# Order of the first transfers and of the first steps in a kernel for sliding-window attention and an ELU feed-forward layer

## The chip, the cores and the metric

The kernel runs on one core of a Trainium2 chip. The metric is the device time of one execution in microseconds (us), as the median of several executions; lower is better. In what follows PE is TensorE (matrix products and transposes), PEld its weight loads, DVE is VectorE, ACT is ScalarE, POOL is GpSimd and SP is SyncE. SP and ACT also issue transfers of the hardware queues, POOL those of the software queue, which may change the type on the way.

## What is computed

Attention with a window of 32 to each side, on 8 batches of 8 heads, 576 positions, head size 64; its output, laid out as 4608 tokens by 512, goes through a feed-forward layer of width 2048 with ELU.

```python
scores = scale * np.matmul(q, k.transpose(0, 1, 3, 2))
mask = np.abs(pos[:, None] - pos[None, :]) <= window
scores = np.where(mask, scores, -1000000000.0)
attn = np.exp(scores - np.max(scores, axis=-1, keepdims=True))
attn = attn / (np.sum(attn, axis=-1, keepdims=True) + 1e-09)
x = np.matmul(attn, v)        # then to (4608, 512)
h = x @ w_in
g = np.where(h > 0.0, h, alpha * (np.exp(np.minimum(h, 0.0)) - 1.0))
out = g @ w_out
```

## The kernel before

All inputs and the output are float32 in HBM; the products run in bfloat16. The kernel has two halves that run interleaved, in an order written out by hand: every engine executes its instructions in the order in which the Python code emits them.

**Attention.** The 576 queries of a batch are nine blocks of 64; two blocks are a "pair" of 128 tokens, so there are 36 pairs. For a pair, `scores` (L281) makes 16 products of keys and queries into PSUM, `exponential` (L296) is one activation on ACT into the tile `pu`, `mask` (L303) a multiplication on DVE with 0/1 masks into `pm`, `pv` (L312) 16 products with the values, `normalize` (L326) a reciprocal and a multiplication on DVE into `x_st`, `x_transpose` (L337) four transposes on PE and `x_evac` (L353) their eviction by ACT into `xT`. The values stand in `V_e`, with an extra column of ones that gives the row sums, and shifted by 64 positions in `V_o`, which `rotate_v` (L137) copies on DVE.

**Queries and keys** must be transposed. `load_qk` (L115) loads them, in halves of a batch (HALF_A, HALF_B; four transfers of 288 KB for q and k together, two of them for each) or whole. `cast_qk` (L236) casts to bfloat16, `transpose_qk` (L266) transposes on PE into PSUM and evicts to `qT` or `kT`. For batch 0, `front_cast` and `front_transpose` (L367, L371) do this in two pieces. HALF_A of batch 0 serves pairs 0 and 1, HALF_B pairs 2 and 3.

**Feed-forward layer.** Two pairs make a tile of 256 tokens; there are 18 tiles and 8 groups of 256 hidden units each, so 144 steps. `mm1(kk)` (L544, "first product of step kk") multiplies w_in with `xT` (eight matmuls of 128x256), ACT takes the exponential (`e_sb`, L565), DVE subtracts one (`m_sb`, L567), and one step later `elu` (L572) makes `g_sb`. `mm2(kk)` (L583, "second product of step kk") multiplies `g_sb` with w_out into PSUM, four matmuls of 128x512. By `order` (L539) steps 0 to 3 take tile 0 and hidden groups 0 to 3, steps 4 to 7 tile 1 and the same groups; steps 8 on take groups 4 to 7. The weights are loaded in quarters by `load_w_in` and `load_w_out` (L153, L160) on POOL's queue, which casts them; quarter c holds groups 2c and 2c + 1. So steps 0 and 1 need quarter 0, step 2 is the first that needs quarter 1, step 8 the first that needs quarter 2.

**Order at the start.** POOL makes the identity and the masks, then issues V's blocks 1, 0, 2 of batch 0, three last mask operations, w_in quarter 0, V's blocks 3 and 4, w_out quarter 0 and so on. SP issues HALF_A of batch 0 (with ACT), then stands at a gate: `gate` (L148) is a transfer of one element whose only purpose is that SP waits until its source is written, here the last mask. After it come the loads of HALF_B, then a gate on w_in's quarter 1, the loads of HALF_A of batch 1, a gate on w_in's quarter 3, and the further loads. On PE `idle` (L376) emits products with zeros in places where PE would wait.

**Loop.** From L609 on, each step kk runs `elu(kk - 1)`, the tasks of slot "dve", `mm1(kk)`, the tasks of slot "mid", the second products (normally of step kk - 2, LAG at L608; exceptions in the table at L618), and the tasks of slot "end". The tasks of the first steps (L452 to L465) hold the transposes of HALF_B and pairs 2 and 3; `swap_pools` at step 4 gives PSUM space of the first pairs to later tiles.

Of the kernel before, what the change touches and what calls it, by code (L numbers as in the profile page):

```python
# [10 lines left out]
BF16 = mybir.dt.bfloat16  # L11
# [4 lines left out]
def _bap(ap, new_ap, off=0):  # L16
    return bass.AP(tensor=ap.tensor, offset=ap.offset + off,
                   ap=[list(x) for x in new_ap])
# [3 lines left out]
def kernel(  # L22
# [9 lines left out]
    nc = tc.nc  # L32

    B, H, S, D = q.shape
# [9 lines left out]
    HP = H // 2  # L44
    NC = 128 // HP
# [69 lines left out]
    def load_qk(b, which, part, engs=(nc.sync, nc.sync)):  # L115
        z, nj = part
        t = lpool.tile([128, 2, nj * D], FP32, tag=f"f{which}{nj}",
                       name=f"f{which}")
        qk_f[b, which, z] = t
        src = (q, k)[which][b, :, z * NC * nj:(z + 1) * NC * nj, :].rearrange(  # L120
            "(g h) (c j) d -> c g h (j d)", h=2, j=nj)
        for h in range(2):
            engs[h].dma_start(out=t[:, h, :], in_=src[:, :, h, :])  # L123

    def load_v(b, m):
        lo = 128 * m - WIN
        p0 = max(0, -lo)
        p1 = min(128, S - lo)
        nc.gpsimd.dma_start(  # L129
            out=V_e[b % 3][p0:p1, m, :, 0:D],  # L130
            in_=v[b, :, lo + p0:lo + p1, :].rearrange("h p d -> p h d"))
# [16 lines left out]
    def gate(src, dt=BF16, eng=nc.sync):  # L148
        gates[0] += 1
        t = cpool.tile([1, 1], dt, name=f"gate{gates[0]}")  # L150
        eng.dma_start(out=t, in_=src)

    def load_w_in(c):  # L153
        w = D_FF // 4
        nc.gpsimd.dma_start(
            out=w_in_sb[:, :, c * w:(c + 1) * w],
            in_=moe_w_in[:, c * w:(c + 1) * w].rearrange(
                "(o p) f -> p o f", p=128))

    def load_w_out(c):  # L160
        n = NFO // 4
        nc.gpsimd.dma_start(
            out=w_out_sb[:, c * n:(c + 1) * n, :],
            in_=moe_w_out[c * n * 128:(c + 1) * n * 128, :].rearrange(
                "(o p) f -> p o f", p=128))

    def w_in_at(c):
        return w_in_sb[0:1, 0, (c + 1) * (D_FF // 4) - 1:(c + 1) * (D_FF // 4)]
# [7 lines left out]
    def edges(i):  # L176
        nc.vector.memset(V_e[i][:, :, :, D:VD], 1.0)
        nc.vector.memset(V_e[i][0:32, 0], 0.0)
        nc.vector.memset(V_e[i][96:128, VS - 1], 0.0)
        if i < 2:  # L180
            for c0, n in ((KPAD - WIN, HP), (KPAD + HP * S, 1)):
                z = kT[i][:, c0:c0 + WIN]
                nc.vector.memset(_bap(z, [z.ap[0], [S, n], [1, WIN]]), 0.0)

    edges(0)
    edges(1)

    ident = cpool.tile([128, 128], BF16)
    make_identity(nc, ident)

# [7 lines left out]
        base=2 * WIN, pattern=[[0, 5], [1, QB]], channel_multiplier=-1)  # L200
    for m in (1, 0, 2):
        load_v(0, m)
    for mi in (0, 4):
        nc.gpsimd.affine_select(
            out=masks[:, mi, :], in_=masks[:, mi, :], compare_op=ALU.is_ge,
            fill=0.0, base=-WIN, pattern=[[0, QB]], channel_multiplier=1)
# [3 lines left out]
        channel_multiplier=-1)  # L210
    kinds = ["FE", "EE", "EL", "LF"]

    gate(masks[0:1, 3, 0:1])
    for which in range(2):
        load_qk(0, which, HALF_B)
    load_w_in(0)
    for m in (3, 4):
        load_v(0, m)
    load_w_out(0)
    load_w_in(1)  # L220
    load_w_out(1)

# [7 lines left out]
    def copy_on(eng, d_, s_):  # L230
        if eng is nc.scalar:
            nc.scalar.copy(d_, s_)  # L232
        else:
            eng.tensor_copy(d_, s_)  # L234
# [12 lines left out]
    def keys_or_queries(b, which):  # L247
        if which == 0:
            return qT[b % 2].rearrange("p g s -> p (g s)")
        return kT[b % 2][:, KPAD:KPAD + HP * S]  # L250
# [12 lines left out]
        nc.sync.dma_start_transpose(  # L263
            out=keys_or_queries(b, which), in_=in_dram.pop((b, which)))

    def transpose_qk(b, which, part, j0, n, evac, tag="t0"):  # L266
        z, nj = part
        src = qk_b[b, which, z]
        pt = ps_tile([128, 1024 if n <= 8 else 2048], BF16, tag, "ptx")
        for j in range(n):  # L270
            nc.tensor.transpose(  # L271
                pt[:, j * 128:(j + 1) * 128], src[:, j0 + j, :], ident)
        d = keys_or_queries(b, which)
        copy_on(evac,
                _bap(d, [d.ap[0], [S, HP], [nj, NC], [1, n]],
                     z * NC * nj + j0),
                _bap(pt, [pt.ap[0], [1, HP], [HP, NC], [128, n]]))

    st = {}

# [15 lines left out]
    def exponential(i):  # L296
        psS = st[i][0]
        pu = apool.tile([128, H, 2 * QB], BF16, tag="pu")
        nc.scalar.activation(  # L299
            pu, _bap(psS, [psS.ap[0], [1, 1024]]), AX.Exp, scale=SCALE)  # L300
        st[i][1] = pu
# [35 lines left out]
    def x_transpose(i):  # L337
        x_st, tag = st[i][3:]
        pt = ps_tile([128, NDO, 128], BF16, tag, "psXT")
        for do in range(NDO):  # L340
            nc.tensor.transpose(
                pt[:, do, :], x_st[:, 2 * do:2 * do + 2, :], ident)
        st[i] = pt
# [9 lines left out]
    def x_evac(i, eng=nc.vector):  # L353
        copy_on(eng, xT_of(i), st.pop(i))
# [12 lines left out]
    def front_cast(which, part, eng):  # L367
        for j0, n in SPLIT:
            cast_qk(0, which, part, j0, n, eng)

    def front_transpose(which, part, evac, tags):  # L371
        for (j0, n), tag in zip(SPLIT, tags):
            transpose_qk(0, which, part, j0, n, evac, tag)


    def idle(n, tag):  # L376
        ps = ps_tile([128, 512], FP32, tag, "ps_idle")
        for _ in range(n):
            nc.tensor.matmul(ps, lhsT=zeros[:, 0:128], rhs=zeros,
                             start=True, stop=True)  # L380
# [12 lines left out]
    for i, tag in ((0, "s"), (1, "u")):  # L393
        scores(i, tag)
        exponential(i)
    idle(4, "y0")
    rotate_v(0, 0, 2)
    for i in (0, 1):
        mask(i)
    pv(0)  # L400
    idle(2, "h0")
    pv(1)
    for i in (0, 1):
        normalize(i)
    for i in (0, 1):
        idle(1, "h1")
        x_transpose(i)
        x_evac(i, nc.scalar)
    idle(2, "h1")
    front_cast(0, HALF_B, nc.scalar)  # L410
    front_cast(1, HALF_B, nc.vector)


    load_w_in(2)
    load_w_out(2)
    for m in range(3):
        load_v(1, m)
    load_w_in(3)
    load_w_out(3)
    for m in range(3, VS):  # L420
        load_v(1, m)
    gate(w_in_at(1))
    for which in range(2):
        load_qk(1, which, HALF_A)
    gate(w_in_at(3))
# [10 lines left out]
    def at(kk, slot, fn, *args):  # L436
        tasks.setdefault((kk, slot), []).append((fn, args))
# [11 lines left out]
        at(kk + 2, "end", x_evac, i, nc.scalar)  # L449


    at(1, "mid", front_transpose, 1, HALF_B, nc.scalar, ("s", "u"))  # L452
    at(1, "mid", front_transpose, 0, HALF_B, nc.vector, ("y0", "y1"))
    at(2, "dve", rotate_v, 0, 2, VS - 1)
    for i, tag in ((2, "s"), (3, "u")):
        at(1, "mid", scores, i, tag)
        at(1, "mid", exponential, i)
        at(2, "dve", mask, i)
    at(2, "dve", lambda: mm2(1))
    for i in (2, 3):  # L460
        at(2, "dve", pv, i)
        at(2, "dve", normalize, i)
        at(3, "mid" if i == 3 else "dve", x_transpose, i)
        at(3, "mid" if i == 3 else "dve", x_evac, i, nc.scalar)
    at(4, "dve", swap_pools)  # L465

    for part, kq in ((HALF_A, 7), (HALF_B, 15)):
# [115 lines left out]
    def mm2(kk):  # L583
        t, s = order[kk]
        if s == 0:
            psY[t] = [ps_tile([128, D_MODEL], FP32, g, "psY")
                      for g in (("h2", "t0") if t == 1 else ("y0", "y1"))]
        g_sb = g_t.pop(kk)
        last = t == NT - 1 and s == STEPS - 1
        for ts in range(2):  # L590
            for j in range(FG):
                nc.tensor.matmul(  # L592
                    psY[t][ts],
                    lhsT=g_sb[:, j, ts * 128:(ts + 1) * 128],
                    rhs=w_out_sb[:, s * FG + j, :],
                    start=(s == 0 and j == 0),
                    stop=(s == STEPS - 1 and j == FG - 1))
        if s == STEPS - 1:
            for ts in range(2):
                z = 1 - ts if last else ts  # L600
                eng = (nc.scalar, nc.vector)[z]
                y_sb = opool.tile([128, D_MODEL], FP32, tag=f"y_sb{z}",
                                  name="y_sb")
                copy_on(eng, y_sb, psY[t][ts])
                (nc.scalar if last and ts else nc.sync).dma_start(
                    out_t[t, :, ts, :], y_sb)

    LAG = 2  # L608
    for kk in range(NSTEP + LAG):  # L609
        run(kk, "first")  # L610
        if 1 <= kk < NSTEP:
            elu(kk - 1)
        run(kk, "dve")
        if kk < NSTEP:
            mm1(kk)
        run(kk, "mid")

        for n in {1: (0,), 2: (), 3: ()}.get(  # L618
                kk, (kk - LAG,) if kk >= LAG else ()):
            mm2(n)  # L620
        run(kk, "end")
# [30 lines left out]
```

The softmax here doesn't subtract the row's maximum and nothing guards it: scores larger than these inputs give would overflow.

## Time and profile before

The median of 13 executions is 312.81 us (311.62 to 315.13). The profile was taken of the execution that lasted 315.13 us, whose span is 313.4 us; the rest lies around the span.

| engine | busy, us | share of the span |
|---|---|---|
| PE | 294.8 | 94% |
| DVE | 246.9 | 79% |
| ACT | 170.7 | 54% |
| POOL | 43.8 | 14% |

| stretch, us | PE busy, us | granted clock of PE | DMA, GB/s |
|---|---|---|---|
| 10 to 15 | 4.42 | 0.90 | 260 |
| 15 to 20 | 3.38 | 1.00 | 218 |
| 20 to 25 | 2.66 | 0.63 | 206 |
| 25 to 30 | 5.00 | 0.69 | 227 |
| 30 to 35 | 4.01 | 1.00 | 267 |
| 60 to 80 | 19.34 | 1.00 | 205 |
| 160 to 240 | 78.13 | 1.00 | 164 |

Some times of the first steps, from the timeline: the first product of step 0 starts at 15.48 us, of step 2 at 27.65, of step 4 at 31.16, of step 6 at 34.63. SP's gate on the masks goes at 6.39, the four loads of HALF_B from 7.19 on; the gate on w_in's quarter 1 at 24.30, the loads of HALF_A of batch 1 from 25.03 on. POOL issues w_in quarter 0 at 6.33, w_out quarter 0 at 8.96, w_in quarter 1 at 9.71. How to read the lines that follow: in the chain of waits a line is a start, a length and what the time went to; in a timeline it is start, busy time, engine, line of the code, operation, the tile written and the tile read, and in brackets how long the engine was idle before and what ended that; in a table of stretches it is the stretch, then busy time (and count) of PE, PEld, DVE, ACT and POOL, the granted clock, the DMA engines' share and GB/s.

### The profile page before, as it was taken

To read this page: it belongs to the slowest core of one execution; us is meant where nothing else is said; L and a number is where in the kernel's file an instruction comes from. 1 tells how busy PE (TensorE), PEld (TensorE's weight loads), DVE (VectorE), ACT (ScalarE), POOL (GpSimd) and SP (SyncE) were. 2 spreads that over 40 slices of the span, in tenths; PEclk is the share of its full clock that TensorE was granted. 3 is DMA by queue.
4 is the path that set the end of the run, shared out by engine and by line. 5 is a ranking of instruction groups with operands and counts; after the bars stand their busy time and mean duration, and the time that the engine had idled before them with its cause. 6 is when DMAs were issued, how large, how long until landed. Compare 5 with 4: busy or idle time off the path is not lost.

```text
span 313.4 us, 7510 instructions
## 1 busy us (share of the span) xinstructions
PE 294.8 (94%) x2996; PEld 198.2 (63%) x3048; DVE 246.9 (79%) x480; ACT 170.7 (54%) x256; POOL 43.8 (14%) x60
## 2 busy tenths in 40 slices
PE   6858999999999999999998999999999999999994
PEld 2445666667666666666665666666666666666662
DVE  6666688799979788888886888888888787776663
ACT  3554556868683775567366735673636353534331
POOL 8633000572102032020202000000000000000000
PEclk9787999999999999999999999999999999999998
DMA  9999999999999999779999996269111111111011
GB/s 189 222 205 239 223 231 356 299 195 188 332 197 173 339 187 176 221 94 255 269 137 168 389 252 159 62 191 188 69 36 67 36 69 35 69 33 69 0 69 68
DMA packets 91657, 52.93 MB, mean 169 GB/s; under 512 B 76518, under 2 KB 80614, under 8 KB 91622
## 3 DMA queue, kind: packets, MB, share of 16 engines
q1 hardware_dynamic: 48022, 36.77, 44.2%
q0 software_dynamic: 41728, 8.92, 38.4%
q10 hardware_dynamic: 1872, 6.75, 6.6%
q8 instruction: 24, 0.39, 0.6%
q14 instruction: 11, 0.09, 0.1%
HBM read 36.70 MB, written 15.34 MB: 166 GB/s over the span
## 4 chain that ended last, share of the span: by engine, by line
PE 81%; DVE 7%; DMA 4%; issue 2%; POOL 2%; ACT 1%; SPq 1%; DVEq 0%; POOLq 0%
PE ps L558 37%; PE psY L592 36%; PE psS L288 3%; PE psS L320 3%; DMA f<-in_k_dram 3%; DVE g_sb L577 2%; DMA xT<-x_st 2%; PE ptx L271 1%; DVE m_sb L567 1%; DVE pm L308 1%; DVE x_st L332 1%; POOL Ve L129 1%; SPq L123 1%; ACT e_sb L565 1%; DVE y_sb L234 1%
## 5 line engine op out<-in xcount | busy, mean ns | idle before, releaser
L565 ACT ACTIVATE e_sb<-ps 128x512 f32<-128x512 f32 (+1 forms) x145 | 86.2, 594 | 122.7 <-PE ps L558 115.5
L558 PE MATMUL ps<-xT,w_in_sb 128*128 128x256 bf16 x1152 | 149.5, 273 | 2.9 <-DVE g_sb L577 1.6
L592 PE MATMUL psY<-w_out_sb,g_sb 128*128 128x512 bf16 x525 | 140.6, 383 | 3.2 <-issue 0.9
L558 PEld LDWEIGHTS <-w_in_sb 128*128 128x128 bf16 x1152 | 110.8, 98 | 41.7 <-issue 3.5
L577 DVE SCALAR_TENSOR_TENSOR g_sb<-ps,m_sb 128x512 bf16<-128x512 f32 (+1 forms) x145 | 99.5, 686 | 12.9 <-PE ps L558 0.5
L567 DVE TENSOR_SCALAR m_sb<-e_sb 128x512 bf16<-128x512 f32 (+1 forms) x145 | 62.7, 433 | 32.7 <-ACT e_sb L565 30.8
L592 PEld LDWEIGHTS <-g_sb 128*128 128x128 bf16 x576 | 54.9, 98 | 39.3 <-issue 1.6
L129 POOL DMA_DIRECT2D Ve<-in_v_dram x40 | 34.9, 887 | 136.2 <-PE psS L320 96.8
L299 ACT ACTIVATE pu<-psS 128x1024 bf16<-128x1024 f32 x36 | 36.5, 1020 | 4.0 <-PE psS L288 4.0
L332 DVE TENSOR_TENSOR x_st<-psS,rc 128x512 bf16<-128x512 f32 x36 | 24.9, 692 | 3.4 <-DMA xT<-x_st 2.2
L232 ACT CAST qkb<-f 128x768 bf16<-128x768 f32 (+3 forms) x32 | 26.7, 837 | 0.0
L308 DVE TENSOR_TENSOR pm<-pu,masks 128x1024 bf16<-128x1024 bf16 x36 | 24.6, 683 | 1.5 <-ACT pu L299 1.5
L320 PEld LDWEIGHTS <-pm 128*64 128x64 bf16 x576 | 11.4, 113 | 10.2 <-DVE pm L308 6.8
L288 PE MATMUL psS<-qT,kT 64*128 64x64 bf16 x576 | 12.7, 196 | 2.6 <-DVE qT L234 2.1
L140 DVE COPY Vo<-Ve 64x1040 bf16<-64x1040 bf16 x32 | 14.2, 444 | 1.0
L288 PEld LDWEIGHTS <-kT 64*128 64x128 bf16 x576 | 10.3, 98 | 7.2 <-issue 5.4
L320 PE MATMUL psS<-Ve,pm 128*64 128x65 bf16 x320 | 13.9, 199 | 0.3 <-DVE pm L308 0.2
L234 DVE COPY y_sb<-psY 128x512 f32<-128x512 f32 x18 | 12.3, 686 | 1.2 <-PE psY L592 1.1
L320 PE MATMUL psS<-Vo,pm 128*64 128x65 bf16 x256 | 12.6, 199 | 0.2 <-DVE pm L308 0.2
L234 DVE CAST qkb<-f 128x1152 bf16<-128x1152 f32 (+3 forms) x14 | 8.5, 627 | 4.9 <-DMA f<-in_k_dram 4.4
L232 ACT COPY y_sb<-psY 128x512 f32<-128x512 f32 x18 | 10.5, 583 | 2.2 <-PE psY L592 2.2
L271 PE MATMUL ptx<-ident,qkb 128*128 128x128 bf16 x108 | 8.4, 225 | 3.2 <-DVE qkb L234 3.2
(32 smaller groups left out, 65.9 us busy)
## 6 DMA issues: line engine op xcount, KB each, us to landing
out_dram<-y_sb SPq DMA_DIRECT2D x35, 256.0 KB, 2.6
f<-in_q_dram SPq DMA_DIRECT2D x12, 576.0 KB, 8.8
f<-in_k_dram SPq DMA_DIRECT2D x12, 576.0 KB, 8.9
in_dram<-qkb ACTq DMA_DIRECT2D x10, 576.0 KB, 5.2
Ve<-in_v_dram POOLq DMA_DIRECT2D x24, 128.0 KB, 7.7
w_in_sb<-in_moe_w_in_dram POOLq DMA_DIRECT2D x4, 512.0 KB, 16.3
w_out_sb<-in_moe_w_out_dram POOLq DMA_DIRECT2D x4, 512.0 KB, 17.5
f<-in_q_dram SPq DMA_DIRECT2D x7, 288.0 KB, 6.0
```

What stands on the lines that cost most here:

```text
L129: nc.gpsimd.dma_start(out=V_e[b % 3][p0:p1, m, :, 0:D], in_=v[b, :, lo + p0:lo + p1, :].rearrange("h p d -> p h d"))
L232: nc.scalar.copy(d_, s_)
L288: nc.tensor.matmul(psS[:, h % 2, hp * 128 + z * QB:hp * 128 + (z + 1) * QB], lhsT=kT[b % 2][base:base + 64, KPAD + hp * S + QB * qb - WIN: ...
L299: nc.scalar.activation(pu, _bap(psS, [psS.ap[0], [1, 1024]]), AX.Exp, scale=SCALE)
L308: nc.vector.tensor_mul(pm, pu, _bap(mm, [mm.ap[0], [0, H], [1, 2 * QB]]))
L320: nc.tensor.matmul(psS[QB * z:QB * (z + 1), par, hp * VD:(hp + 1) * VD], lhsT=pm[:, par * HP + hp, z * QB:(z + 1) * QB], rhs=vv[:, qb // 2 ...
L332: nc.vector.tensor_mul(x_st, _bap(psS, [psS.ap[0], [VD, HP], [512, 2], [1, D]]), _bap(rc, [rc.ap[0], [2, HP], [1, 2], [0, D]]))
L558: nc.tensor.matmul(ps[:, j, :], lhsT=w_in_sb[:, do, fo * 128:(fo + 1) * 128], rhs=xT[t][:, :, do, :], start=(do == 0), stop=(do == NDO - 1))
L565: nc.scalar.activation(e_sb, ps, AX.Exp)
L567: nc.vector.tensor_scalar(m_sb, e_sb, -1.0, None, ALU.add)
L577: nc.vector.scalar_tensor_tensor(g_t[kk][:, z * w:(z + 1) * w, :], ps, 0.0, m_t[kk][z], ALU.max, ALU.min)
L592: nc.tensor.matmul(psY[t][ts], lhsT=g_sb[:, j, ts * 128:(ts + 1) * 128], rhs=w_out_sb[:, s * FG + j, :], start=(s == 0 and j == 0), stop=( ...
```

## The change

- The identity is made ahead of the memsets of V and kT in the code; on each engine alone the order stays.
- SP's first gate waits for the last memset of kT (DVE) in place of the last mask operation (POOL); the four loads of HALF_B of batch 0 stand behind it.
- POOL issues w_in quarter 0 ahead of the three last mask operations, w_out quarter 0 ahead of V's blocks 3 and 4, and V's blocks 0 and 1 of batch 1 ahead of w_in's quarter 2.
- SP's second gate, ahead of HALF_A of batch 1, waits for the first exponential (`pu` of pair 0) in place of w_in's quarter 1.
- The casts and transposes of HALF_B go ahead of step 0: q's casts stand ahead of the xT evictions on ACT, q's transposes between those of pairs 0 and 1 on PE, with evictions on ACT (before: DVE) deferred behind both xT evictions; k's transposes follow, with evictions on DVE (before: ACT).
- Five of the twenty products with zeros are left out.
- The value products of pairs 2 and 3 go behind the first product of step 2; their normalization goes to step 3, their transposes around the second product of step 2.
- Second products 2 and 3 run in steps 3 and 4 (before: 4 and 5).

```diff
@@ -182,11 +182,16 @@
                 z = kT[i][:, c0:c0 + WIN]
                 nc.vector.memset(_bap(z, [z.ap[0], [S, n], [1, WIN]]), 0.0)
 
+    ident = cpool.tile([128, 128], BF16)
+    make_identity(nc, ident)
+
+
+
     edges(0)
     edges(1)
-
-    ident = cpool.tile([128, 128], BF16)
-    make_identity(nc, ident)
+    gate(kT[1][0:1, KPAD - 1:KPAD])
+    for which in range(2):
+        load_qk(0, which, HALF_B)
 
 
 
@@ -200,6 +205,7 @@
         base=2 * WIN, pattern=[[0, 5], [1, QB]], channel_multiplier=-1)
     for m in (1, 0, 2):
         load_v(0, m)
+    load_w_in(0)
...
@@ -210,13 +216,9 @@
         channel_multiplier=-1)
     kinds = ["FE", "EE", "EL", "LF"]
 
-    gate(masks[0:1, 3, 0:1])
-    for which in range(2):
-        load_qk(0, which, HALF_B)
-    load_w_in(0)
+    load_w_out(0)
     for m in (3, 4):
         load_v(0, m)
-    load_w_out(0)
     load_w_in(1)
     load_w_out(1)
 
...
@@ -263,18 +265,25 @@
         nc.sync.dma_start_transpose(
             out=keys_or_queries(b, which), in_=in_dram.pop((b, which)))
 
-    def transpose_qk(b, which, part, j0, n, evac, tag="t0"):
+    def transpose_qk(b, which, part, j0, n, evac, tag="t0", later=None):
         z, nj = part
         src = qk_b[b, which, z]
         pt = ps_tile([128, 1024 if n <= 8 else 2048], BF16, tag, "ptx")
         for j in range(n):
             nc.tensor.transpose(
                 pt[:, j * 128:(j + 1) * 128], src[:, j0 + j, :], ident)
-        d = keys_or_queries(b, which)
-        copy_on(evac,
-                _bap(d, [d.ap[0], [S, HP], [nj, NC], [1, n]],
-                     z * NC * nj + j0),
-                _bap(pt, [pt.ap[0], [1, HP], [HP, NC], [128, n]]))
+
+        def evict():
+            d = keys_or_queries(b, which)
+            copy_on(evac,
+                    _bap(d, [d.ap[0], [S, HP], [nj, NC], [1, n]],
+                         z * NC * nj + j0),
+                    _bap(pt, [pt.ap[0], [1, HP], [HP, NC], [128, n]]))
+
+        if later is None:
+            evict()
+        else:
+            later.append(evict)
 
...
@@ -368,9 +377,9 @@
         for j0, n in SPLIT:
             cast_qk(0, which, part, j0, n, eng)
 
-    def front_transpose(which, part, evac, tags):
+    def front_transpose(which, part, evac, tags, later=None):
         for (j0, n), tag in zip(SPLIT, tags):
-            transpose_qk(0, which, part, j0, n, evac, tag)
+            transpose_qk(0, which, part, j0, n, evac, tag, later)
...
@@ -393,33 +402,39 @@
     for i, tag in ((0, "s"), (1, "u")):
         scores(i, tag)
         exponential(i)
+    st0 = st[0][1]
     idle(4, "y0")
     rotate_v(0, 0, 2)
     for i in (0, 1):
         mask(i)
     pv(0)
-    idle(2, "h0")
+    idle(1, "h0")
     pv(1)
     for i in (0, 1):
         normalize(i)
-    for i in (0, 1):
-        idle(1, "h1")
-        x_transpose(i)
-        x_evac(i, nc.scalar)
-    idle(2, "h1")
     front_cast(0, HALF_B, nc.scalar)
+    evictions = []
+    x_transpose(0)
+    x_evac(0, nc.scalar)
+    front_transpose(0, HALF_B, nc.scalar, ("y0", "y1"), evictions)
+    x_transpose(1)
+    x_evac(1, nc.scalar)
+    for evict in evictions:
+        evict()
     front_cast(1, HALF_B, nc.vector)
-
-
+    front_transpose(1, HALF_B, nc.vector, ("s", "u"))
+
+
+    for m in (0, 1):
+        load_v(1, m)
     load_w_in(2)
     load_w_out(2)
-    for m in range(3):
-        load_v(1, m)
+    load_v(1, 2)
     load_w_in(3)
     load_w_out(3)
     for m in range(3, VS):
         load_v(1, m)
-    gate(w_in_at(1))
+    gate(st0[0:1, 0, 0:1])
     for which in range(2):
         load_qk(1, which, HALF_A)
     gate(w_in_at(3))
...
@@ -449,19 +464,16 @@
         at(kk + 2, "end", x_evac, i, nc.scalar)
 
 
-    at(1, "mid", front_transpose, 1, HALF_B, nc.scalar, ("s", "u"))
-    at(1, "mid", front_transpose, 0, HALF_B, nc.vector, ("y0", "y1"))
+    at(2, "dve", lambda: mm2(1))
     at(2, "dve", rotate_v, 0, 2, VS - 1)
     for i, tag in ((2, "s"), (3, "u")):
         at(1, "mid", scores, i, tag)
         at(1, "mid", exponential, i)
         at(2, "dve", mask, i)
-    at(2, "dve", lambda: mm2(1))
-    for i in (2, 3):
-        at(2, "dve", pv, i)
-        at(2, "dve", normalize, i)
-        at(3, "mid" if i == 3 else "dve", x_transpose, i)
-        at(3, "mid" if i == 3 else "dve", x_evac, i, nc.scalar)
+        at(2, "mid", pv, i)
+        at(3, "dve", normalize, i)
+        at(3, "mid" if i == 2 else "end", x_transpose, i)
+        at(3, "mid" if i == 2 else "end", x_evac, i, nc.scalar)
     at(4, "dve", swap_pools)
...
@@ -615,7 +627,7 @@
             mm1(kk)
         run(kk, "mid")
 
-        for n in {1: (0,), 2: (), 3: ()}.get(
+        for n in {1: (0,), 2: (), 3: (2,), 4: (3,), 5: ()}.get(
                 kk, (kk - LAG,) if kk >= LAG else ()):
             mm2(n)
         run(kk, "end")
```

## The prediction

> **What bounds the kernel now.** I read the page first: TensorE (PE) is busy 94% of the span and reads 9 tenths in almost every slice, except the first three (6, 8, 5). What can be won or lost by an edit of the first transfers lies there. Next the chain of waits from 9 us on:
>
> ```profile
> 9.89 8.30 DMA f<-in_k_dram
> 18.19 0.02 issue
> 18.22 0.83 DVE qkb L234 x2
> ...
> 20.72 1.36 DVE qT L234 x2
> 22.08 0.04 issue
> 22.12 1.04 PE psS L288 x32
> 23.16 0.54 PE psY L592
> ...
> 26.69 1.03 PE psS L320 x29
> 27.71 1.20 PE ps L558 x8
> ```
>
> The end hangs on the last load of the second half of k: it lands at 18.2 us, is cast, transposed and evicted until 22.1, and only then do the scores of pairs 2 and 3 (L288) go, after them the second products of steps 0 and 1 (L592), the value products (L320), and at 27.65 the first product (L558) of step 2. Third, GpSimd's (POOL's) own timeline, because its waits tell when the weights land: the bracket names the transfer that released it.
>
> ```profile
> 15.28 0.79 POOL L129 DMA_DIRECT2D Ve<-in_v_dram  x1 [2.58 <-DMA w_in_sb<-in_moe_w_in_dram]
> ...
> 22.05 0.75 POOL L155 DMA_DIRECT2D w_in_sb<-in_moe_w_in_dram  x1 [0.68 <-DMA w_out_sb<-in_moe_w_out_dram]
> 24.57 0.74 POOL L162 DMA_DIRECT2D w_out_sb<-in_moe_w_out_dram  x1 [1.76 <-DMA w_in_sb<-in_moe_w_in_dram]
> 27.11 0.88 POOL L129 DMA_DIRECT2D Ve<-in_v_dram  x1 [1.80 <-DMA w_out_sb<-in_moe_w_out_dram]
> ```
>
> So quarter 0 of w_in is there by about 15, quarter 0 of w_out by about 21.8, quarter 1 of w_in by 24.3 (SP's gate on it goes at 24.30), quarter 1 of w_out by 27. Step 2 is the first to use quarter 1 of w_in: it has 27.65 - 24.3 = 3.3 us of slack, no more. Fourth, the DMA queues over 19 to 28 us, when only GpSimd's queue (q0) moves, and over 29 to 33 us, when the loads of q and k (q1, issued by SP) run beside it:
>
> ```profile
> q0 software_dynamic: 1872, 1.86, 124.3%
> ...
> q1 hardware_dynamic: 490, 1.02, 75.3%
> q0 software_dynamic: 552, 0.21, 42.2%
> ```
>
> (packets, MB, share of 16 engines). Alone q0 moves 1.86 MB in 9 us, 206 GB/s; beside q1 0.21 MB in 4 us, 52 GB/s. A load of q and k stops the weights almost entirely. Last, the granted clock in stretches around the idle time:
>
> ```profile
> 17.86:21.27 3.41, 1.23 (x18) 1.10 (x19) 2.94 (x6) 1.53 (x3) 1.65 (x2) 1.00 1.32 202
> 21.27:24.70 3.43, 2.36 (x35) 1.46 (x36) 2.92 (x6) 1.93 (x2) 0.98 (x3) 0.50 1.24 206
> 24.70:28.10 3.40, 3.40 (x40) 1.75 (x39) 1.42 (x3) 0.01 (x1) 1.49 (x2) 0.50 1.24 206
> ```
>
> After a stretch in which PE works 1.23 of 3.41 us, its clock is 0.50 for the next two.
>
> [...]
>
> **The change, part by part.** I follow one mark: the start of the first product of step 6, at 34.63 us in the timeline of before. There both kernels have the same products behind them (first products 0 to 5, second products 0 to 3), and from there on the order is the same on every engine.
>
> 1. *Second half of q and k earlier.* SP's gate waited for the last mask operation and went at 6.39; now it waits for the last memset of kT, which ends at about 4.6. The four loads go some 1.7 us earlier, and meet V's small packets rather than w_in in the queue: before, q1 moved only the gate's 2 packets between 8.5 and 11 us although its loads were issued from 7.19. I expect k to land at 14.5 to 16 instead of 18.2.
>
> 2. *Its transposes ahead of step 0.* 18 transposes (1.23 us) and the casts (0.83 on DVE, 1.25 on ACT, which now stand ahead of the two xT evictions in ACT's order) go before the first product of step 0. Before, that product started at 15.48, on the xT eviction. Now, with k landed at about 14.6: cast to 15.4, transposes to 16.2; at 16.2 to 17 step 0 starts, 0.7 to 1.5 us later. Then steps 0 and 1 (1.91), scores (1.04), and second products 0 and 1 (4 x 0.215 us each at full clock, 1.75 for both): if nothing else held it, step 2 could start at 16.2 + 4.7 = 20.9, not 27.65. The eviction of qT that stood behind m_sb and g_sb on DVE (20.64 to 22.07) is out of the way.
>
> 3. *Gate of batch 1's first half: pu of pair 0 instead of quarter 1 of w_in.* The first exponential ends at about 11.0, so these four loads (1.18 MB) are issued from 11.7 instead of 25.03, and stand in q1 right behind the second half of batch 0. In the queues of the chip they are now ahead of the end of w_in quarter 0, of w_out quarter 0, V's blocks 3 and 4, and w_in quarter 1. Price: over 28.5 to 34.5 us, where they ran before, q0 moved 0.47 MB in 6 us; at 206 GB/s it would have been 1.24 MB. The 0.77 MB are 3.7 us; as part of it is V, slower by itself, I take 3.2 (bounds 3.0 and 3.7). On the credit side w_in quarter 0 is issued 0.9 us earlier (5.4 instead of 6.33) and the stretch from 8.5 to 11 us, where q0 moved only 0.31 MB (125 GB/s, 1.0 us short of its own pace), is filled by q1. I take 0.9 (bounds 0 and 1.4). Quarter 1 of w_in then lands at 24.3 + 3.2 - 0.9 = 26.6 (25.9 to 28.0). Call it T: step 2 starts at T, 5.7 us after PE could have.
>
> 4. *w_out quarter 0 ahead of V's blocks 3 and 4.* It lands at 20.5 to 23.5, V at 23 to 25 by the same reckoning; second products, rotation (0.88) and masks (2 x 0.69) end before T or with it. Cost nothing while T is the last; if V came 2 us later, the value products would be held by that.
>
> 5. *After T.* The value products of pairs 2 and 3 now stand behind the first product of step 2, and their normalization behind g_sb of step 2 on DVE. With the latencies of the timeline (first product to end of g_sb: 31.16 to 34.08, 2.92): g_sb of step 2 ends at T + 2.92; reciprocal and x_st of pair 2 0.94, of pair 3 0.85: T + 4.7. Transposes of pair 2 0.3, second product of step 2 0.86, transposes of pair 3 to about T + 5.45, eviction on ACT to T + 6.1, where step 4, which reads this xT, begins. From step 4 to step 6 before took 3.47 with two second products; one of these (0.86) is already done, but step 6 needs the bank that g_sb of step 4 frees, 2.95 after step 4's start. The mark is at T + 9.05; before it was 27.65 + 6.98.
>
> 6. *Clock.* PE idles before T (about 22.5 to 26.6), so the stretch after it is granted half: the first product and value products at half cost 0.2 to 0.4 more; I take 0.3. Five warm-up products less (L379) cost nothing by themselves.
>
> 7. *V of batch 1 (blocks 0, 1) before quarter 2 of w_in.* It moves that quarter to about T + 6.6 = 33.2; its first use is step 8, after 38. Nothing.
>
> Sum: 26.6 + 9.05 + 0.3 = 35.95 against 34.63: 1.3 us slower. Against the profiled execution's own 315.13 us (span 313.4) this is 316.4; that execution was the slowest of the 13, 2.3 above their median, so at the median it is 312.81 + 1.3 = 314.1. Bounds of T, 25.9 and 28.0, give +0.6 and +2.7; without the clock term +0.3: 313.1 to 315.5.
>
> **Rivals.** *The weights land in time.* The mark equals that of before at T = 34.63 - 9.05 = 25.6; below it the change wins. If q1 has so much of its work done in the poorly used stretch before 11 us, or takes its turns so, that quarter 1 of w_in keeps its old place or comes 0.9 earlier (24.3 to 23.4), the mark is at 33.35 to 32.45: 1.3 to 2.2 faster, 311.5 to 310.6. For it: the long wait for k is removed without doubt, and SP's loads can't have cost q0 what it didn't use. Against it: the two queue lines, and that the sum of bytes ahead of quarter 1 grows by 1.18 MB. *The loads of batch 1 start late* (before, q1's loads first moved 3.5 to 4 us after their issue, 7.19 to about 11.3 and 25.03 to about 28.5): then half of their cost falls behind quarter 1, T is about 25, and the time is 0.3 to 0.6 faster, about 312.4: no change. *V is hit.* If SP's earlier loads hold back V's first blocks, rotation, masks and step 0 come later; it would take 5 us of it before it shows, as T comes last. Price 0 until then; 1 us for each above.
>
> **How the numbers follow.** Forecast (weights late) 0.60, weights in time 0.30, loads late 0.10. A measurement of this kernel can tell about 0.3%, 0.94 us, from no change. Of the forecast's 0.60 about 0.52 lie above +0.94 and 0.08 within; of the second 0.28 faster, 0.02 within; of the third 0.05 faster, 0.04 within, 0.01 slower. Together 0.33 faster, 0.14 same, 0.53 slower. Range: from 310.6 (the second rival's better end) to 315.8, the forecast's end and 0.3 for the clock's chance; the forecast's own is 313.1 to 315.5.
>
> **What would show it.** Right: GpSimd's waits show quarter 1 of w_in landing at 26 to 28; PE's first product of step 2 waits for it with PE idle for over 2 us before; k's second half lands before 16; q1 is busy from about 8 to 20 us. Wrong: step 2 starts before 25.6, or waits for V or masks rather than for w_in; then the queue's sharing, step 3 of the sum, is what failed.

## The result, and the profile after

The changed kernel takes 314.69 us (median of 11 runs, 313.80 to 315.34), the kernel before, run beside it, 312.55 (48 runs, 310.66 to 315.13): a ratio of 1.0069 with a 95% interval of 1.0047 to 1.0090. It is 2.1 us slower. The profiled execution took 315.23 us (span 313.5).

The page of the changed kernel, its engine line, the engine shares of its chain, and the row of the first products (the last column is PE's idle time ahead of them and what ended most of it):

```profile
PE 292.6 (93%) x2990; PEld 197.1 (63%) x3043; DVE 246.9 (79%) x480; ACT 170.5 (54%) x256; POOL 44.1 (14%) x60
...
PE 83%; DMA 5%; DVE 5%; POOL 3%; issue 2%; ACT 1%; DVEq 0%; POOLq 0%
...
L570 PE MATMUL ps<-xT,w_in_sb 128*128 128x256 bf16 x1152 | 151.0, 275 | 4.7 <-DMA w_in_sb<-in_moe_w_in_dram 3.3
```

PE is as busy as before, to one per cent; the reader should look at the end of the last line: 3.3 of the 4.7 us are one wait for a quarter of w_in. The chain of waits of the changed kernel from 9.7 us on shows where it stands:

```profile
9.71 16.18 DMA w_in_sb<-in_moe_w_in_dram
25.90 0.05 issue
25.94 1.89 PE ps L570 x8
27.83 1.03 PE psS L329 x31
28.86 1.82 PE ps L570 x8
30.68 0.55 PE psXT L350 x4
```

In the kernel before this stretch hung on the second half of k; now it hangs on quarter 1 of w_in, which lands at 25.89, and the first product of step 2 (25.94) follows 0.05 us later. PE's own timeline of the changed kernel (bracket: idle before, and what ended it):

```profile
20.80 1.89 PE L604 MATMUL psY<-w_out_sb,g_sb 128*128 128x512 bf16 x7 [1.43 <-DMA w_out_sb<-in_moe_w_out_dram]
25.94 1.89 PE L570 MATMUL ps<-xT,w_in_sb 128*128 128x256 bf16 x8 [3.26 <-DMA w_in_sb<-in_moe_w_in_dram]
...
28.79 1.89 PE L570 MATMUL ps<-xT,w_in_sb 128*128 128x256 bf16 x8
...
36.27 1.03 PE L570 MATMUL ps<-xT,w_in_sb 128*128 128x256 bf16 x8 [0.20 <-DVE g_sb L589]
```

The last line is the mark, the first product of step 6, at 36.27 us. The two 1.89 are first products of 8 matmuls at a granted clock of 0.50 (25.0 to 31.6 us); at 1.00 they take 1.03 to 1.05. The second half of k, which the kernel before waited for until 18.2, is there early, as DVE's timeline of the changed kernel shows:

```profile
15.77 0.83 DVE L236 CAST qkb<-f 128x640 bf16<-128x640 f32 x2 [1.89 <-DMA f<-in_k_dram]
```

SP's queue and GpSimd's timeline of the changed kernel, one fence each, show what stands ahead of that weight:

```profile
10.11 0.63 SPq L151 DMA_DIRECT2D gate<-pu  x1
10.84 1.20 SPq L123 DMA_DIRECT2D f<-in_q_dram  x2
```

```profile
21.04 0.74 POOL L162 DMA_DIRECT2D w_out_sb<-in_moe_w_out_dram  x1 [5.08 <-DMA w_out_sb<-in_moe_w_out_dram]
23.81 1.11 POOL L129 DMA_DIRECT2D Ve<-in_v_dram  x1 [2.03 <-DMA Ve<-in_v_dram]
24.91 0.76 POOL L155 DMA_DIRECT2D w_in_sb<-in_moe_w_in_dram  x1
26.18 0.74 POOL L162 DMA_DIRECT2D w_out_sb<-in_moe_w_out_dram  x1 [0.51 <-DMA w_in_sb<-in_moe_w_in_dram]
```

The gate on pu lets batch 1's first loads of q and k go from 10.84. Quarter 0 of w_out is there at about 21, V's last blocks at about 23.8, quarter 1 of w_in by 25.9. The queues of the changed kernel over 11 to 20 us (packets, MB, share of 16 engines):

```profile
q1 hardware_dynamic: 881, 1.81, 59.2%
q0 software_dynamic: 932, 0.82, 55.1%
```

GpSimd's queue moves 0.82 MB in 9 us, 91 GB/s, against 206 when it was alone (the kernel before, 19 to 28 us). The two queues moved about as many packets in this stretch, 881 and 932; a packet of q1 is 2054 B and one of q0 880 B (bytes over packets), so q and k got more than twice the bytes. Not every stretch shows equal counts: in the kernel before q1 had 382 packets over 13 to 16 us and q0 828, of about 160 B, with 0.78 and 0.13 MB. That q and k took the larger part of the bytes is measured in both. Last, the granted clock (third number from the right) in the stretches of the changed kernel that the prediction looked at:

```profile
17.86:21.27 3.41, 1.92 (x43) 1.43 (x42) 2.54 (x5) 3.02 (x4) 0.23 (x1) 1.00 1.50 268
21.27:24.70 3.43, 1.42 (x6) 0.45 (x5) 1.08 (x3) 0.00 (x0) 1.40 (x2) 1.00 1.41 201
24.70:28.10 3.40, 2.16 (x20) 1.38 (x22) 1.06 (x2) 0.23 (x1) 1.71 (x3) 0.53 1.67 186
```

The idle time falls into the second stretch and the half clock into the third, in which step 2 starts.

One more reading is needed before anything is compared. The two profiled spans, 313.4 and 313.5, are nearly equal, although the medians differ by 2.1. The waits of the kernel before over steps 60 to 80 (147.85 to 187.58 us; total, times, longest) name one part of the reason:

```profile
DVE x_st L332 <- DMA xT<-x_st: 2.2, 2, 1.4
```

That stretch took 39.73 us there and 38.33 in the changed kernel. The wait is not in every execution: the kernel before profiled again (e0, below) doesn't show it over 146 to 185 us, and takes 279.2 us from the mark to its time, against 280.5. So the profile of before that the prediction was made from has about 1.3 us in it, far behind the mark, that the second profile doesn't have.

### The profile page after: what moved, and what is told of

It reads as the page before. It is cut to its first block, busy times and chain, and to the rows that moved or that the text cites. A ratio compares the mean times of both kernels' runs of the same rounds, so it can differ in the third digit from the quotient of the medians.

```text
span 313.5 us, 7500 instructions
## 1 busy us (share of the span) xinstructions
PE 292.6 (93%) x2990; PEld 197.1 (63%) x3043; DVE 246.9 (79%) x480; ACT 170.5 (54%) x256; POOL 44.1 (14%) x60
## 4 chain that ended last, share of the span: by engine, by line
PE 83%; DMA 5%; DVE 5%; POOL 3%; issue 2%; ACT 1%; DVEq 0%; POOLq 0%
PE ps L570 38%; PE psY L604 36%; DMA w_in_sb<-in_moe_w_in_dram 5%; PE psS L329 3%; PE psS L297 3%; DVE g_sb L589 1%; PE ptx L273 1%; POOL Ve L129 1%; DVE pm L317 1%; PE psXT L350 1%; DVE m_sb L579 1%; DVE x_st L341 1%; DVE y_sb L236 1%; ACT e_sb L577 1%; DVE Vo L140 0%
## 5 line engine op out<-in xcount | busy, mean ns | idle before, releaser
L341 DVE TENSOR_TENSOR x_st<-psS,rc 128x512 bf16<-128x512 f32 x36 | 24.9, 692 | 1.2
L297 PEld LDWEIGHTS <-kT 64*128 64x128 bf16 x576 | 9.5, 95 | 5.2 <-issue 4.2
L297 PE MATMUL psS<-qT,kT 64*128 64x64 bf16 x576 | 11.9, 191 | 0.7 <-DVE kT L236 0.7
```

Source lines behind the costliest of these rows:

```text
L297: nc.tensor.matmul(psS[:, h % 2, hp * 128 + z * QB:hp * 128 + (z + 1) * QB], lhsT=kT[b % 2][base:base + 64, KPAD + hp * S + QB * qb - WIN: ...
L341: nc.vector.tensor_mul(x_st, _bap(psS, [psS.ap[0], [VD, HP], [512, 2], [1, D]]), _bap(rc, [rc.ap[0], [2, HP], [1, 2], [0, D]]))
```

## The experiments

The theory: the four early loads of batch 1 (1.18 MB) delay the weights, and the new order of steps 2 to 5, with value products and normalization behind step 2's first product, makes all of that work wait with it. The rival: the new order, or the moved transposes, costs the time whatever the weights do. All ratios are to the kernel before, run beside each, with 95% intervals.

One difference holds them together. Time minus mark is 278.96 to 278.98 us in the profiled executions of the changed kernel and of e1, e3, e4, e5, e6, e7 and e10, and 279.1 to 279.6 in e0, e2, e8 and e9. Whatever differs between the first eight is decided before the start of step 6. Where half clock is said of a part of e0 to e10, it is read from the pace of the matmuls: in the changed kernel 8 of 128x256 take 1.89 us at a granted clock of 0.50, in the kernel before 16 take 1.91 at 1.00.

**e1, the gate alone put back**

```diff
-    gate(st0[0:1, 0, 0:1])
+    gate(w_in_at(1))
```

> The changed kernel with one thing undone: SP's second gate waits for quarter 1 of w_in again, not for pu of pair 0. Theory (batch 1's early loads hold back the weights): quarter 1 of w_in lands 3.2 us sooner than the 25.9 of the changed kernel, at 22.7 (22 to 24); step 2 starts there, step 6 starts at 32 to 34 instead of 36.27, and the time falls by 2.3 to 3.3 us, to 311.4 to 312.4, ratio to before 0.996 to 1.000. Rival (the order behind it costs it: transposes ahead of step 0, value products behind step 2's first product): w_in is no longer waited for, but the time stays at 314 or above, ratio 1.005 or more.

311.01 us (22 runs), 0.9955 [0.9937, 0.9972]. The chain of waits of e1:

```profile
9.62 12.96 DMA w_in_sb<-in_moe_w_in_dram
22.57 0.05 issue
22.62 1.06 PE ps L570 x8
...
31.59 1.03 PE ps L570 x8
```

Quarter 1 of w_in lands at 22.57, 3.3 us before that of the changed kernel, at the same place in GpSimd's order. The mark follows 8.97 us after step 2. One line of the change carries the loss, and without it the rest is a gain over the kernel before.

**e2, the same line alone in the kernel before**

```diff
+    st0 = st[0][1]
...
-    gate(w_in_at(1))
+    gate(st0[0:1, 0, 0:1])
```

> The kernel before with one thing of the change: the second gate waits for pu of pair 0. Theory: the same loads delay quarter 1 of w_in by about 3 us to 26.5 to 27.7, but there step 2 starts at 27.65 anyway, on the chain of k's second half, so the slack of 3.3 us swallows nearly all: ratio to before 0.999 to 1.004. Rival (early loads cost their 3 us whatever stands beside them): ratio 1.008 to 1.011.

314.85 us (9 runs), 1.0077 [1.0049, 1.0104]: a miss, and near the rival's number. PE's timeline of e2:

```profile
24.87 3.56 PE L593 MATMUL psY<-w_out_sb,g_sb 128*128 128x512 bf16 x8 [2.85 <-DMA w_out_sb<-in_moe_w_out_dram]
...
29.00 1.05 PE L559 MATMUL ps<-xT,w_in_sb 128*128 128x256 bf16 x8
...
35.77 1.04 PE L559 MATMUL ps<-xT,w_in_sb 128*128 128x256 bf16 x8
```

The expectation counted the slack of quarter 1 of w_in. What came last was another weight in the same queue: quarter 0 of w_out, 3 us later than before (24.8 against 21.8), with both second products, at half clock (3.56 us for 8 matmuls; four take 1.03 in step 4), and the value products behind it. Quarter 1 of w_in, landed at 27.3, was hidden behind that. The loads cost the kernel before about as much as the changed one, by another wait.

**e0, the kernel before once more**

> The kernel before itself, profiled once more. In its first profile the first product of step 6 starts at 34.63 us, and between steps 60 and 80 there is a wait of 2.2 us of DVE for the transfers of xT that none of the other traces has (39.7 us for these 20 steps against 38.3). If that wait is of that one execution alone, the 20 steps take 38.3 to 38.5 here and the time is near the median, 312 to 313; if it belongs to the kernel, 39.5 or more.

312.27 us (one run). PE's timeline of e0, first products of step 2 and of step 6:

```profile
26.32 1.05 PE L558 MATMUL ps<-xT,w_in_sb 128*128 128x256 bf16 x8
...
33.09 1.04 PE L558 MATMUL ps<-xT,w_in_sb 128*128 128x256 bf16 x8
```

The mark is at 33.09 where the first profile had 34.63. The eight matmuls of the second products 0 and 1 take 2.78 us here and took 3.5 there, where the granted clock was 0.50 from 21.3 to 28.15 us. The 32 scores ahead of them (21.99 here, 22.12 there) take 1.04 in both, and 0.64 at a granted clock of 1.00 in the changed kernel (18.73), so the half clock was on here as well; about four of the eight matmuls at 0.43 us each and the rest at 0.215 make the 2.78, so by this estimate it ended at about 24.7.

**e3, the clock kept up through the wait**

```diff
     at(2, "dve", lambda: mm2(1))
+    at(2, "dve", idle, 12, "h0")
```

> The changed kernel with 12 products of zeros (2.6 us at full clock) put on PE ahead of the first product of step 2, where it idles 3.3 us for w_in. Theory (the half clock after that idle time is 1.0 to 1.3 us of the loss): step 2 still starts at 25.9, its matmuls take half as long, from step 2 to step 6 about 9.1 us instead of 10.33; time 1.0 to 1.3 below the changed kernel, 313.4 to 313.7, ratio to before 1.003 to 1.004. Rival (DVE's and ACT's chain of normalization sets that stretch, the clock doesn't matter): 0 to 0.3 us, ratio 1.006 to 1.008.

314.02 us (19 runs), 1.0049 [1.0029, 1.0070]. PE's timeline of e3:

```profile
23.04 2.75 PE L388 MATMUL ps_idle<-zeros 128*128 128x512 bf16 x12
26.86 1.05 PE L571 MATMUL ps<-xT,w_in_sb 128*128 128x256 bf16 x8 [1.06 <-DMA w_in_sb<-in_moe_w_in_dram]
...
28.48 1.05 PE L571 MATMUL ps<-xT,w_in_sb 128*128 128x256 bf16 x8
...
35.83 1.03 PE L571 MATMUL ps<-xT,w_in_sb 128*128 128x256 bf16 x8 [0.21 <-DVE g_sb L590]
```

With 12 products of zeros in the idle time the two first products take 1.05 instead of 1.89, and the mark is 8.97 after step 2 instead of 10.33. So in the profiled execution the half clock cost 1.36 us. In the medians it is 0.67 us (314.69 to 314.02), and the two intervals overlap. The granted clock, averaged over an execution, is below 1.00 in every timed execution of the changed kernel (0.975 to 0.998, median 0.989); with the products of zeros its median is 0.995, and 6 of 19 executions have 1.00. So most executions of the changed kernel pay something; how much behind step 2 isn't settled. The weights are no earlier here (step 2 starts at 26.86), and most of the loss stays.

**e4 and e6, steps 2 to 5 in the old order, with either gate**

```diff
-        at(2, "mid", pv, i)
-        at(3, "dve", normalize, i)
...
+        at(2, "dve", pv, i)
+        at(2, "dve", normalize, i)
...
-        for n in {1: (0,), 2: (), 3: (2,), 4: (3,), 5: ()}.get(
+        for n in {1: (0,), 2: (), 3: ()}.get(
```

e4 has this and e1's gate, e6 this and the changed kernel's gate on pu.

> The changed kernel with the second gate on quarter 1 of w_in and the steps 2 to 5 as before (value products of pairs 2 and 3 ahead of the first product of step 2, second products two steps behind); the earlier second half of q and k and its transposes ahead of step 0 stay. Theory: k and weights are both early, value products are done by about 23.5, step 2 starts at 23 to 24, step 6 about 7 us later at 30 to 31 against 34.63; 2.5 to 3.5 us below before, ratio 0.989 to 0.992. Rival (the gain is given back at step 6, since batch 1's loads are then late for their casts, or V's blocks 3 and 4 hold the masks): ratio 0.996 to 1.000.

> The changed kernel, gate on pu and all, with steps 2 to 5 as before: value products of pairs 2 and 3 ahead of the first product of step 2, second products two steps behind. Theory (the loss has a second part: what stands behind step 2's first product is late by the whole wait for w_in): the value products fit into that wait, step 2 starts at 25.9 to 26.5, step 6 about 7 us later at 33 to 33.5 instead of 36.27, and the time is 1.5 to 2.5 us below the changed kernel: 312.2 to 313.2, ratio 0.999 to 1.002. Rival (the order of the steps doesn't matter, as with the gate back it didn't): 314 to 315, ratio 1.005 to 1.008.

e4: 311.06 us (13 runs), 0.9943 [0.9921, 0.9966], no better than e1, a miss. PE's timeline of e4:

```profile
17.41 3.07 PE L571 MATMUL ps<-xT,w_in_sb 128*128 128x256 bf16 x16
...
25.19 1.05 PE L571 MATMUL ps<-xT,w_in_sb 128*128 128x256 bf16 x8
```

Step 2 starts at 25.19, since the 16 matmuls of steps 0 and 1 take 3.07 us, the larger part at half clock, and the value products ahead of step 2 wait for rotation and masks until 24.2; the mark follows 6.78 later: what is won behind step 2 is lost in front of it.

e6: 312.53 us (14 runs), 0.9991 [0.9964, 1.0018], as expected. Its chain of waits:

```profile
8.96 14.80 DMA Ve<-in_v_dram
...
24.48 1.31 DVE pm L317 x2
...
26.28 0.99 PE ps L571 x8
```

V's last block comes at 23.8, rotation and masks end at 25.8, and quarter 1 of w_in, hardly earlier than in the changed kernel, has landed at about 25.7. Late V and late w_in wait beside each other, the value products and normalization are done before step 2 (26.21), and the mark (32.99) is 3.3 us ahead of that of the changed kernel. The four together:

| | gate on quarter 1 of w_in | gate on pu |
|---|---|---|
| old order of steps 2 to 5 | e4: 0.9943 | e6: 0.9991 |
| new order | e1: 0.9955 | changed kernel: 1.0069 |

The early loads cost 0.48% (1.5 us) under the old order and 1.14% (3.6 us) under the new one. The second is clear of the noise; the first is at its edge, as the intervals of e4 and e6 just touch (0.9966 and 0.9964). The new order costs nothing measurable unless the weights are late.

**e7 and e5, between the two gates**

e7 lets q's two loads go at pu, and k's two at quarter 1 of w_in; e5 lets all four go at quarter 0 of w_in.

```diff
     gate(st0[0:1, 0, 0:1])
-    for which in range(2):
-        load_qk(1, which, HALF_A)
+    load_qk(1, 0, HALF_A)
+    gate(w_in_at(1))
+    load_qk(1, 1, HALF_A)
```

```diff
-    gate(st0[0:1, 0, 0:1])
+    gate(w_in_at(0))
```

> The changed kernel with half of the dose: behind the gate on pu only q's two loads of batch 1, and k's two behind a gate on quarter 1 of w_in. Theory (the bytes of q and k ahead of the weights are the cost, about 3.2 us for four loads): quarter 1 of w_in lands halfway between 22.6 (gate back) and 25.9 (all four early), at 24.0 to 24.6; the time is halfway too, 312.4 to 313.2, ratio 0.999 to 1.003. Rival (what costs is that any load stands there at all, or a wait of SP): as the changed kernel, 1.006 or more.

> The changed kernel with the second gate on quarter 0 of w_in instead of pu of pair 0, so that the same four loads of batch 1 are issued at about 15.7 instead of 10.8. Theory: they meet the tail of w_out quarter 0 and all of V's blocks 3, 4 and of w_in quarter 1, which lands at 24.3 to 25.5, between 22.6 and 25.9; time 312.3 to 313.7, ratio 0.999 to 1.004. Rival (a late enough gate is as good as one on quarter 1): 311 to 311.5, ratio 0.995 to 0.997.

e7: 312.48 us (14 runs), 1.0004 [0.9980, 1.0027]; e5: 312.83 us (14 runs), 1.0003 [0.9974, 1.0031]. Step 2's wait in PE's timeline of e7:

```profile
25.26 1.05 PE L571 MATMUL ps<-xT,w_in_sb 128*128 128x256 bf16 x8 [2.11 <-DMA w_in_sb<-in_moe_w_in_dram]
```

In the medians half of the bytes, or later bytes, give about half of the loss. In the profiled executions e5 fits that: step 2 starts at 24.48, between 22.62 (e1) and 25.94 (changed), though there the second products end only just before, behind matmuls of steps 0 and 1 at half clock (the last seven on record take 1.70 us). e7's time was as expected, but in the profiled execution its w_in came at 25.2, outside the 24.0 to 24.6 expected; that execution took 313.50, 1.0 above e7's median.

**e8, normalization before g_sb**

```diff
-        at(3, "dve", normalize, i)
-        at(3, "mid" if i == 2 else "end", x_transpose, i)
-        at(3, "mid" if i == 2 else "end", x_evac, i, nc.scalar)
+        at(2, "end", normalize, i)
+        at(3, "mid", x_transpose, i)
+        at(3, "mid", x_evac, i, nc.scalar)
```

(on top of e1)

> The kernel with the gate back on w_in, and on DVE the normalization of pairs 2 and 3 ahead of g_sb of step 2, the transposes of both pairs ahead of the second product of step 2. Theory (after step 2 starts, the order on DVE sets when xT is ready for step 4): from step 2 to step 4 about 4.9 instead of 5.99 us, 0.8 to 1.1 us faster than with the gate back alone: 309.9 to 310.3, ratio 0.991 to 0.993. Rival (PE or the weights set it): 310.8 to 311.2, ratio 0.994 to 0.996.

310.78 us (20 runs), 0.9943 [0.9922, 0.9964]: a miss, at the number of its rival and not to be told from e1. PE's timeline of e8:

```profile
27.80 1.04 PE L604 MATMUL psY<-w_out_sb,g_sb 128*128 128x512 bf16 x4 [0.20 <-DVE g_sb L589]
28.68 1.04 PE L570 MATMUL ps<-xT,w_in_sb 128*128 128x256 bf16 x8
```

xT of pair 2 is early, but now g_sb of step 2 is late, and the second product that waits for it holds PE until 28.66, when step 4 may start: 5.36 us after step 2 instead of 5.99, where 4.9 was expected. The mark follows 8.34 after step 2, 0.63 earlier than in e1. Behind it the profiled execution loses 0.66 us against e1 (279.63 from mark to time). Over the 40 us from 51.66 DVE was busy 35.36 us, over those from 51.59 in e1 34.87; why isn't known. So one execution gained 0.63 at the mark, which the medians can't show.

**e9, q and k late again**

```diff
-    gate(kT[1][0:1, KPAD - 1:KPAD])
-    for which in range(2):
-        load_qk(0, which, HALF_B)
...
+    gate(masks[0:1, 3, 0:1])
+    for which in range(2):
+        load_qk(0, which, HALF_B)
     load_w_out(0)
```

(on top of e1)

> The kernel with the second gate back on w_in, and the first gate back on the masks too, so that the second half of q and k is issued from about 8 us on instead of 5.4. Theory (with the weights in time, the chain of k's second half is what is left, as its transposes stand ahead of step 0): k lands at 18 to 18.6 instead of 15.8, step 0 starts at 19 to 19.7 instead of 17.1, and the time is 1.5 to 2.5 us above the kernel with only the second gate back: 312.5 to 313.5, ratio 1.000 to 1.003. Rival (the early loads of the second half gain nothing, the weights set the pace): 311 to 311.4, ratio 0.995 to 0.997.

316.12 us (6 runs), 1.0102 [1.0058, 1.0146]: the right sign, at 1.5% above e1 (4.6 us) about twice the size. The waits of e9 over its first 25 us (total, times, longest):

```profile
DVE qkb L236 <- DMA f<-in_k_dram: 6.3, 1, 6.3
ACT qkb L234 <- DMA f<-in_q_dram: 5.1, 1, 5.1
```

k's cast goes at 20.50. The gate ahead of its loads waits for the masks again, which now stand behind w_in's issue on GpSimd; what else holds the loads isn't settled. As the transposes now stand ahead of step 0, everything stands behind it: step 0 starts at 21.99, and its and step 1's 16 matmuls take 3.62 us at half clock instead of 1.91. The early loads of the second half are worth these 4.6 us to this order of the work: without them, though the second gate waits for quarter 1 of w_in again, it is 1.0% slower than the kernel before.

**e10, GpSimd's order of issue as before**

```diff
-    load_w_in(0)
...
-    load_w_out(0)
+    load_w_in(0)
     for m in (3, 4):
         load_v(0, m)
+    load_w_out(0)
...
-    for m in (0, 1):
-        load_v(1, m)
     load_w_in(2)
     load_w_out(2)
-    load_v(1, 2)
+    for m in range(3):
+        load_v(1, m)
```

(on top of e1; quarter 0 of w_in again behind the masks)

> The kernel with only the second gate back, and POOL's issues in the order of before: the last masks ahead of w_in quarter 0, V's blocks 3 and 4 ahead of w_out quarter 0, V of batch 1 behind quarter 2 of the weights. Theory: the bytes ahead of quarter 1 of w_in are the same, so it lands at 22.5 to 23.3 as before; w_out quarter 0 lands 1.5 us later, at 20.4, where step 0's second product wants it; the time is within 0.5 us of the kernel with only the gate back: 310.8 to 311.5, ratio 0.995 to 0.997. Rival (the order on POOL carries the gain): 312 or more, ratio 0.999 or more.

310.80 us (16 runs), 0.9946 [0.9921, 0.9971], as e1. Step 2 waits for its weight until 23.20, the mark is at 32.17. That part of the change carries nothing that can be measured.

e1, e4, e8 and e10 beat both kernels by about the same; none of them can be told from the others.

## Why the prediction was right

The sign, the cause and the time (314.69 in 313.1 to 315.5) were right. By its steps:

1. *Second half of q and k earlier*: right. k's cast on DVE starts at 15.77, in the 14.5 to 16 given.
2. *Transposes ahead of step 0*: right for step 0, which starts at 16.89 (16.2 to 17). The free start of step 2, 20.9, was too early: the second products wait for g_sb, and in e1 they end at 22.3. It changed nothing in the sum, as the weight comes last, but the price of the late weight is then 25.94 - 22.3 = 3.6 us, not 5.7.
3. *The gate*: right, and shown by e1 from one side and by e2 from the other. T was 25.9, the early bound of its range, where 26.6 was taken, and just ahead of the 26 to 28 named as the sign. The price was right, 3.3 us against e1 where 3.2 was taken. The credit was too small: quarter 1 of w_in lands at 22.57 in e1 and at 24.3 in the profile of before, 1.7 us where 0.9 was taken and 1.4 was the bound (in e10, where it lands at about 23.15, it is 1.1; all of these are single executions). And the queue of the weights was not stopped almost entirely: it moved 91 GB/s beside q and k.
4. *w_out and V*: right for the changed kernel (20.8 and 23.8). That quarter 0 of w_out could decide in its turn was not seen; e2 showed it, in the kernel before.
5. *After T*: 9.05 was right at full clock: 8.97 in e1, e3 and e10, 9.01 in e5.
6. *Clock*: the term that was mis-sized. 0.3 was taken for the first product and the value products; it is 1.36 in the profiled execution (10.33 less 8.97), because the half clock also reached step 3, its neighbours and the second product of step 2. The granted clock was 0.50 from 24.9 to about 31.7 us. Between the two profiles of the kernel before its end differed: 28.15 in the first, about 24.7 in e0 (estimated above from its matmuls).
7. *V of batch 1 ahead of quarter 2*: nothing, as said; e10 agrees for GpSimd's order as a whole.

The errors of 3 (-0.7) and 5 with 6 (+1.0) nearly cancel: mark at 36.27 against 35.95. What remains of the difference between the forecast rise of 1.3 and the measured 2.1 lies in the base. The mark of before was taken from its profile, 34.63, and the difference put on the median, as if all of the 2.3 us by which that execution exceeded the median lay behind the mark. In e0, at 312.27, the mark is at 33.09: about 1.5 of it lay ahead of the mark, and 1.3 behind it, for which the wait in steps 60 to 80 stands. Against e0 the mark of the changed kernel is 3.2 us later; the medians differ by only 2.1 because the profiled execution of the changed kernel lies 0.5 above its median, e0 lies 0.3 below that of its kernel, and 0.2 is won back behind the mark. So the mechanism was right, and that the time came within 0.6 us of the forecast's 314.1 is partly luck. The breakeven T of 25.6 moves with it, to 33.09 - 8.97 = 24.1, and e5 with 24.48 and no measurable change fits that, not the other.

Of the rivals, "weights in time" is what e1 has, with another gate; its time lies in the 310.6 to 311.5 of that rival, but quarter 1 of w_in (22.57) and the mark (31.59) were both earlier than the rival has them. "Loads late" fell: q1 moved 1.81 MB between 11 and 20 us, and of batch 1's 1.18 MB only 0.10 was left after 20. "V is hit" cost the changed kernel nothing, since V came at 23.8 and w_in behind it; under the old order of steps it is V that sets the start of step 2 (e6).

## What to carry to other kernels

A load that waits for nothing is not free because its engine is idle: before a gate is moved forward, list what in every queue now stands behind its bytes, all of it and not only the tile whose slack was measured (e2: 0.77%, 2.4 us). Where weights may come late, put ahead of the first instruction that needs them whatever doesn't; the old order of steps 2 to 5 saved 0.78% (2.4 us) in that way (e6 against the changed kernel), and cost nothing that could be measured where the weights were in time (e4 against e1). And before a difference is put on a median, profile the kernel before a second time: one execution's mark was off by 1.5 us.

## What was not expected of the hardware

An idle time of 3.26 us ahead of step 2 cost another 1.36 us behind it in granted clock in the profiled execution, and with 12 products of zeros in that place the half clock did not come (e3). When the half clock ends differs between executions of one kernel: it ended at 28.15 us in the first profile of the kernel before and, by the estimate from its matmuls, at about 24.7 in e0. What sets it was not shown. And a DVE wait of 2.2 us for a transfer of xT in steps 60 to 80 showed in the first profile of the kernel before, and not in the second.
